# Row lists, gates and row stores of an attention, expert and dense chain rewritten; a third of a weight conversion moved to the expert stage

## The chip, the cores and the metric

The kernel runs on one core of one Trainium2 chip. The metric is the time of one execution on the device in microseconds (us); the median of three runs is 1482.52 us (1481.54 to 1482.77).

## The reference, cut to what matters

Three layers follow one another on 4 x 448 = 1792 tokens of 768 values (12 heads of 64): an attention whose heads are mixed before and after the softmax, a layer in which each token goes through one of eight experts, and a dense layer.

```python
scores = scale * q @ k.T                      # per batch and head
scores = einsum('bhij,hg->bgij', scores, w_pre)
attn = softmax(scores)                        # over j
attn = einsum('bhij,hg->bgij', attn, w_post)
x = (attn @ v) as rows of 768                 # 1792 rows
...
logits = xn @ en.T / tau                      # 8 experts, xn and en normalized
expert_idx = argmax(logits, axis=1)
gate_w = softmax(logits)[chosen]              # one number above 0 per token
for e in range(E):
    mask = expert_idx == e
    h = np.maximum(x[mask] @ w1[e], 0.0)
    out[mask] = gate_w[mask, None] * (h @ w2[e])
...
h = x @ w_in
g = h - np.tanh(h)
return g @ w_out
```

`w_in` and `w_out` come in 64-bit floats, so the kernel first makes 32-bit floats of them ("the conversion"). Nothing between gate and output of an expert depends on the gate but by a factor above 0, so a gate may also multiply x ahead of the two products.

## The kernel before, in words

All matrix products of the second and third layer run as three passes over a high and a low part ("h" and "l" tiles, split by an ACT copy and a subtraction), so each split costs one ACT and one DVE (or POOL) instruction. The order on every engine is the order of the program: the schedule is written out by hand, and each engine and each DMA queue (SP's, ACT's, POOL's) works through its list in order.

**Attention stage** (up to about 560 us). 180 blocks of ten rows by twelve heads are run through a loop of steps (L1122); a table of side work by step holds the loads, the transposes, the scores and the conversion. The conversion is cut into 96 pieces of 128 x 256 values (L106 to L134): one load by SP, three DVE instructions on the bits (L128 to L130), three POOL instructions (L131 to L133) and one store by SP. All 96 are in this stage (CONV_A = NCV, L113). x is stored to `x_d` in DRAM in the order in which the attention holds its rows (`emit_X`, L473); that order differs from the tokens', so the kernel keeps two numberings: `tokf` for gathering from `x_d`, `rowg` for the row of the output.

**Expert stage** (about 560 to 934 us). Nine items: experts 0 to 6, one overflow block of 128 tokens ("o"), expert 7 (L909). An expert takes up to 256 tokens. Each item n has a first half, eight chunks f of w1 (`h_chunk`, L787: 18 matmuls, then ACT's relu L796 and DVE's subtraction L797, in two PSUM banks by turns), and a second half, eight chunks of w2 (`y_turned`, L741: 18 matmuls each). After each chunk of the second half come pieces of a to-do list for item n+1 (L1214 to L1224): six splits of w1 (`do1`, L949, then L715 on ACT and L717 on DVE), then four transposes of gathered rows with their split (`xsplit`, L728: three PE transposes L732, ACT L735, DVE L736). The list is dealt out evenly over the chunks that are left. Chunk f also splits w2 chunk f+4 (`do2`, L954) ahead of the list. Four raw buffers of each weight are loaded ahead by SP.

Beside this, the generator `tables` (L915) is pumped a few steps per chunk (L1207 to L1210): first `emit_G` (L571, the gates), then `emit_ov` (L591), which computes each token's place in the list of tokens sorted by expert, sends row number and gate there by sixteen indirect DMAs of POOL into `sid_d` (L674 to L677), reads the list back by a DMA on ACT's queue (L680), makes `sid` and writes the gates in list order to `gat_d` (L687, ACT's queue too).

An item's result is copied by ACT into `yT` at a column that a register holds (`y_out_turned`, L770); the overflow block's goes through `y_out_tokens` (L774). Experts are written in ascending order, 256 columns each, so that what one writes too far the next overwrites.

**Dense stage** (about 934 us to the end). Two halves of 896 columns, each with eight groups of w_in and w_out. Ahead of a half, its columns are multiplied by their gates and split (`y_start`, `y_piece`, L1246 to L1258): a broadcast load of the gates from `gat_d`, and per piece of 128 x 448 the multiplication by POOL (or DVE, L1256), ACT's copy (L1257) and the subtraction (L1258). Twelve pieces run at the start of the stage, twelve spread over the last two groups of the first half. `stageA` (L1297) makes h and its function g with six ACT and DVE steps per tile (L1315 to L1329, POOL's L1295), `stageB` (L1335) the product with w_out, summed up by DVE in `acc` (L1352). The finished rows, 128 at a time, go to `out` by an indirect DMA of POOL (L1355), seven per half; each of them waits until the one before has landed, since any could write any row.

```python
            todo = []
            if not last:
                nw1, nx = [], xtile(f"i{n + 1}")
                todo = [lambda c=c: do1(n + 1, c, nw1) for c in range(KD)]
                todo += [lambda j=j, t=t, hf=hf: xsplit(nx, t, j, hf, f"i{n + 1}") for j, t in enumerate(nxg) for hf in range(2)]
            pts = y_banks(nm, 2 if e == OV else 3)
            for f in range(KF):
                (y_tokens if e == OV else y_turned)(pts, hhl, w2c[f], f)
                if f + W2B < KF:
                    do2(n, f + W2B, w2c)
                k_ = -(-len(todo) // max(1, KF - 1 - f))
                for fn in todo[:k_]:
                    fn()
                todo = todo[k_:]
```

Of the kernel before, what the change touches and what calls it, by code (L numbers as in the profile page):

```python
# [30 lines left out]
def body(ctx: ExitStack, tc, q, k, v, w_pre, w_post, emb, tau, w1, w2, win, wout, out):  # L31
# [42 lines left out]
    sid_d = dram.tile([NT, 2], F32, name="sid_d")  # L74
    gat_d = dram.tile([1, NT], F32, name="gat_d")
# [4 lines left out]
    rowg = persist.tile([128, 4 * B, 2], F32, name="rowg")  # L80
# [32 lines left out]
    CONV_A = NCV  # L113
# [24 lines left out]
    if True:  # L138
# [67 lines left out]
        for b in range(B):  # L206
            pool.iota(tokf[:, 4 * b:4 * b + 4], pattern=[[120, 4]], base=b * S, channel_multiplier=1,
                      allow_small_or_imprecise_dtypes=True)
        dve.tensor_copy(tokh, tokf)
# [17 lines left out]
        rg4 = rowg.rearrange("p (b t) o -> p b t o", b=B)  # L227
        dve.tensor_scalar(rg4[:, :, 0:3, 0], rowf[:, :, 0:3], rq[:, 1:2], None, ALU.add)
        dve.tensor_scalar(rg4[:, :, 3, 0], rowf[:, :, 3], rq[:, 3:4], None, ALU.add)
# [242 lines left out]

        def emit_X(T, hf, cpy=act.copy):  # L473
# [11 lines left out]
            def evac():  # L485
                cpy(xm[:n, hf * 384:(hf + 1) * 384].rearrange("p (c m) -> p c m", c=3), pv[:, :, 0:128])
                dve.reduce_sum(lg[:n, hf, T, :], pv[:, :, 128:136].rearrange("p c e -> p e c"), axis=AX.X)
                r0 = b * S + i0
                if T == 4 * B - 1:
                    act.dma_start(x_d[r0:r0 + n, hf * 384:(hf + 1) * 384], xm[:n, hf * 384:(hf + 1) * 384])  # L490
                elif hf:
                    sp.dma_start(x_d[r0:r0 + n, :], xm[:n])
# [78 lines left out]
        def emit_G():  # L571
# [16 lines left out]
            dve.tensor_copy(rowg[:, :, 1], gate)  # L588
            yield

        def emit_ov():  # L591
# [39 lines left out]
            dve.tensor_copy(z[:, 0:1], bs[:, 0, E - 1:E])  # L631
# [6 lines left out]
            bt = small([128, 4 * B, E], F32, "bt")  # L638
            bz = small([128, 2, 4 * B], F32, "bz")
            for x in range(2):  # L640
                dve.tensor_tensor(bt, ohk, bs[:, x:x + 1, 0:E].to_broadcast([128, 4 * B, E]), op=ALU.mult)
                yield
                dve.reduce_sum(bz[:, x, :], bt, axis=AX.X)
                yield
# [4 lines left out]
            yield  # L649

            dve.tensor_add(bz[:, 0, :], bz[:, 0, :], posk)
            yield

            lo = bz[:, 1, :]
            dve.scalar_tensor_tensor(lo, posk, -float(CAP), lo, ALU.add, ALU.add)
            yield
            ge = small([128, 4 * B], F32, "ge")
            dve.tensor_scalar(ge, lo, c0, mainc[:, E - 1:E], ALU.is_ge, ALU.mult)
            yield
            dve.tensor_add(lo, lo, ge)  # L660
            yield
            dve.tensor_scalar(lo, lo, z[:, 0:1], None, ALU.add)
            yield
            dve.tensor_sub(lo, lo, bz[:, 0, :])
            yield
            dve.tensor_scalar(ge, posk, float(CAP), None, ALU.is_ge)
            yield
            dve.tensor_mul(lo, lo, ge)
            yield
            spos = small([128, 4 * B], I32, "spos")  # L670
            dve.tensor_tensor(spos, bz[:, 0, :], lo, op=ALU.add)
            yield

            for t in range(4 * B):  # L674
                n = IT[t % 4][1]
                pool.indirect_dma_start(out=sid_d, out_offset=bass.IndirectOffsetOnAxis(ap=spos[:n, t:t + 1], axis=0),
                                        in_=rowg[:n, t, :], in_offset=None)  # L677
                yield
            sg = small([128, NT // 128, 2], F32, "sg")
            act.dma_start(sg, sid_d.rearrange("(t p) o -> p t o", p=128))  # L680
            yield
            dve.tensor_copy(sid, sg[:, :, 0])
# [9 lines left out]
    with mctx:  # L692
# [492 lines left out]
        for c in range(4, KD):  # L1185
            feed1(act)
# [265 lines left out]
```

## Time and profile before

| what | value |
|---|---|
| median of three runs | 1482.52 us |
| the profiled execution, its own time | 1482.83 us |
| its span in the profile | 1481.1 us |
| PE busy | 1326.2 us (90%) |
| DVE busy | 1004.2 us (68%) |
| ACT busy | 753.4 us (51%) |
| POOL busy | 514.8 us (35%) |
| mean granted clock of TensorE | 0.954 of full speed |

The span is what the profile covers; the execution's own time is 1.73 us longer. Busy shares are means over three stages with different limits. Clocks are shares of TensorE's full 2.4 GHz. Matmul records overlap, since the engine is pipelined: the distance of two starts is the time that one takes from the engine.

### The profile page before, as it was taken

Reading aid. Unit: us, or ns where it says so; the run is one execution under the profiler, and the core shown is the slowest. Engines: PE = TensorE matmul, PEld = TensorE weight load, DVE = VectorE, ACT = ScalarE, POOL = GpSimd, SP = SyncE. Lnnn points to the kernel's source line nnn. Section 1 sums busy time; section 2 is a strip of 40 time slices with the busy share of each in tenths; the row PEclk is TensorE's granted clock in tenths of the full one; section 3 lists DMA queues with packets and bytes.
Section 4 is the critical chain, followed back from the end, with each engine's and each line's share of the span. In section 5 each row is a group of like instructions: output and inputs, shape, how many; then the busy total and the mean of one; then the engine's idle time right before and its main releaser. Section 6 shows DMA issues by size and latency. Waiting matters only on the chain. (4 is left out here: it accounts for less than half of the span.)

```text
span 1481.1 us, 25663 instructions
## 1 busy us (share of the span) xinstructions
PE 1326.2 (90%) x9422; PEld 1151.0 (78%) x9422; DVE 1004.2 (68%) x2194; ACT 753.4 (51%) x1518; POOL 514.8 (35%) x537
## 2 busy tenths in 40 slices
PE   8989998998999987719999998689999888999994
PEld 5767766776676766719999988569999777999994
DVE  5877886787678765406555564288886758788883
ACT  6666655665666643404454464355444435544440
POOL 0434443444444331120000010454345445444432
PEclk9999999999999998959999999779999999999997
DMA  6765775677566453605655562112212012221101
GB/s 163 209 189 172 217 206 144 189 228 206 159 199 208 151 190 118 192 1 193 214 192 193 193 213 84 56 43 64 65 43 68 31 54 107 65 65 43 44 21 75
DMA packets 145606, 194.98 MB, mean 132 GB/s; under 512 B 57126, under 2 KB 109270, under 8 KB 145478
## 3 DMA queue, kind: packets, MB, share of 16 engines
q1 hardware_dynamic: 137040, 177.73, 39.5%
q0 software_dynamic: 2992, 12.21, 2.2%
q10 hardware_dynamic: 5446, 3.37, 0.8%
q8 instruction: 76, 1.25, 0.3%
q14 instruction: 52, 0.43, 0.1%
HBM read 131.12 MB, written 23.61 MB: 104 GB/s over the span
## 5 line engine op out<-in xcount | busy, mean ns | idle before, releaser
L430 PEld LDWEIGHTS T<-w,p 120*112 120x112 f32 (+1 forms) x1440 | 166.4, 177 | 66.9 <-issue 47.6
L430 PE MATMUL T<-w,p 120*112 120x120 f32 (+1 forms) x1440 | 185.9, 272 | 6.3 <-DVE w L408 3.0
L398 ACT ACTIVATE p<-P,mx 120x448 f32<-120x448 f32 x180 | 113.8, 632 | 110.7 <-DVE mx L405 99.9
L393 PE MATMUL P<-sr,wpre 120*120 120x448 f32 x360 | 167.2, 546 | 1.1 <-DMA sr<-ssb 0.8
L1346 PE MATMUL o<-woh,gh 128*128 128x384 f32 x448 | 151.6, 338 | 12.6 <-DVE acc L1352 12.6
L1309 PE MATMUL h<-yh,wih 128*128 128x448 f32 x384 | 147.7, 385 | 14.6 <-ACT yh L1257 12.8
L395 DVE TENSOR_REDUCE mx<-P 120x1 f32<-120x448 f32 x180 | 111.7, 621 | 68.5 <-PE P L393 67.1
L1295 POOL TENSOR_TENSOR gl<-th,gh 128x448 fp32r<-128x448 f32 x64 | 74.7, 1167 | 234.2 <-ACT gh L1294 196.3
L133 POOL TENSOR_TENSOR cm<-cm,ct 128x256 f32<-128x256 f32 x96 | 69.8, 728 | 246.3 <-DVE ct L130 212.6
L1348 PE MATMUL o<-woh,gl 128*128 128x384 f32 x448 | 151.1, 337 | 4.8 <-POOL gl L1295 4.8
L1347 PE MATMUL o<-wol,gh 128*128 128x384 f32 x448 | 150.5, 336 | 0.0
L1310 PE MATMUL h<-yT,wih 128*128 128x448 f32 x384 | 147.9, 385 | 1.0 <-POOL yT L1258 1.0
L793 PE MATMUL hi<-xhi,w1hi 128*128 128x256 f32 x384 | 110.1, 287 | 42.8 <-DVE hli L797 42.5
L1311 PE MATMUL h<-yh,wil 128*128 128x448 f32 x384 | 146.3, 381 | 2.2 <-POOL wil L1284 1.8
L1352 DVE TENSOR_TENSOR acc<-acc,o 128x384 f32<-128x384 f32 x196 | 106.7, 548 | 43.5 <-PE o L1348 43.5
L1315 ACT ACTIVATE u<-h 128x448 f32<-128x448 f32 x64 | 34.7, 543 | 175.6 <-PE h L1311 175.6
L750 PE MATMUL ypi<-hhi,w2hi 128*128 128x256 f32 x384 | 110.6, 288 | 0.0
L435 ACT COPY A<-T 112x480 f32<-112x480 f32 x180 | 101.4, 563 | 17.3 <-PE T L430 16.8
L794 PE MATMUL hi<-xli,w1hi 128*128 128x256 f32 x384 | 109.1, 284 | 0.0
L795 PE MATMUL hi<-xhi,w1li 128*128 128x256 f32 x384 | 108.8, 283 | 0.0
L752 PE MATMUL ypi<-hhi,w2li 128*128 128x256 f32 x384 | 108.7, 283 | 0.0
L751 PE MATMUL ypi<-hli,w2hi 128*128 128x256 f32 x384 | 108.5, 283 | 0.0
(272 smaller groups left out, 3358.8 us busy)
## 6 DMA issues: line engine op xcount, KB each, us to landing
sr<-ssb SPq DMA_DIRECT2D x176, 210.0 KB
r<-in_moe_w SPq DMA_DIRECT2D x72, 384.0 KB
r<-in_moe_w SPq DMA_DIRECT2D x52, 512.0 KB
craw<-in_moe_w_in SPq DMA_DIRECT2D x48, 256.0 KB
craw<-in_moe_w_out SPq DMA_DIRECT2D x48, 256.0 KB
raw<-wi_d SPq DMA_DIRECT2D x15, 768.0 KB
wor<-wo_d SPq DMA_DIRECT2D x15, 768.0 KB
wi_d<-cm SPq DMA_DIRECT2D x48, 128.0 KB
```

The lines of the kernel that those rows point to most:

```text
L393: pe.matmul(pt[:n, :S], wpre[:n, :n], t[:n, :], start=True, stop=True)
L395: dve.tensor_reduce(mx[:n, 0:1], pt[:n, :S], op=ALU.max, axis=AX.X, negate=True)
L398: return lambda: act.activation(p[:n, :], pt[:n, :S], AF.Exp, bias=mx[:n, 0:1], scale=1.0, accum_out=mx[:n, 1:2])
L430: pe.matmul(pt[:CP, c * n:(c + 1) * n] if m == 10 else pv[:, c], p[:n, c * CP:(c + 1) * CP], w[:n, :] if m == 10 else wv, start=True, stop ...
L750: pe.matmul(o, wh[:, sl], a, start=False, stop=False)
L793: pe.matmul(pt[:, :256], wh[:, sl], xh[:, c, :], start=c == 0, stop=False)
L1309: pe.matmul(pt[:, :S], wi[0][:, c, sl], yh[:, c, :], start=c == 0, stop=False)
L1310: pe.matmul(pt[:, :S], wi[0][:, c, sl], yl[:, c, :], start=False, stop=False)
L1311: pe.matmul(pt[:, :S], wi[1][:, c, sl], yh[:, c, :], start=False, stop=c == KD - 1)
L1346: pe.matmul(pt[:, :384], gh[:, sl], wo[0][:, f, n0:n0 + 384], start=f == 0, stop=False)
L1347: pe.matmul(pt[:, :384], gh[:, sl], wo[1][:, f, n0:n0 + 384], start=False, stop=False)
L1348: pe.matmul(pt[:, :384], gl[:, sl], wo[0][:, f, n0:n0 + 384], start=False, stop=f == GF - 1)
```

## The change

- **Row lists.** The sixteen indirect writes, the read back, `rowg`, `sid`'s conversion and the second numbering are gone. x is stored in the tokens' order (a store with a rearranged DRAM side, one more store for each fourth tile), so one list of indices serves gathers and outputs. Each item's list (256 or 128 row numbers, as integers) is written to `sid_d` by one DMA on ACT's queue at the item's column, after its result. `sid` is loaded from there by SP in the third group of the dense stage.
- **Gates.** They are stored in the tokens' order to `gate_d` by twenty DMAs on ACT's queue (elements of 4 bytes). For each item POOL gathers one gate per token (one or two indirect DMAs), and DVE multiplies the gathered x by it in place, ahead of the transposes: two instructions of 128 x 768 per expert, put in the to-do list between the six splits of w1 and the four `xsplit`. Expert 0 starts before the gates are there: its result waits in PSUM and is multiplied by a row of gates (turned by two matmuls) on the way to `yT`, by DVE, in the first half of item 1. The dense stage multiplies nothing.
- **Row stores.** The fourteen indirect stores go to views of `out` that are declared disjoint, so none waits for another.
- **Conversion.** 64 of the 96 pieces stay in the attention stage; 32 go to the first halves of the eight expert items, after chunks 1, 3, 5 and 7.
- The memory reserved for POOL's DMA descriptors is set to 8192 bytes a partition.

```diff
-    CONV_A = NCV
+    CONV_A = 64
...
+        def x_store(eng, T, xm, cs):
+            b, it = divmod(T, 4)
+            i0, n = IT[it]
+            r0, nb = b * S + i0, n // 10
+            eng.dma_start(x_d[r0:r0 + 10 * nb, cs].rearrange("(m r) d -> r m d", r=nb), xm[:10 * nb, cs])
+            if n % 10:
+                eng.dma_start(x_d[r0 + 10 * nb:r0 + n, cs], xm[10 * nb:n, cs])
...
             dve.reciprocal(gate, es)
             yield
-            dve.tensor_copy(rowg[:, :, 1], gate)
-            yield
+            yield
+            for T in range(4 * B):
+                bq, it = divmod(T, 4)
+                i0, n = IT[it]
+                r0, nb = bq * S + i0, n // 10
+                act.dma_start(gate_d[r0:r0 + 10 * nb].rearrange("(m r) o -> r (m o)", r=nb), gate[:10 * nb, T:T + 1])
+                if n % 10:
+                    act.dma_start(gate_d[r0 + 10 * nb:r0 + n], gate[10 * nb:n, T:T + 1])
+                if T % 4 == 3:
+                    yield
...
-            for t in range(4 * B):
-                n = IT[t % 4][1]
-                pool.indirect_dma_start(out=sid_d, out_offset=bass.IndirectOffsetOnAxis(ap=spos[:n, t:t + 1], axis=0),
-                                        in_=rowg[:n, t, :], in_offset=None)
-                yield
-            sg = small([128, NT // 128, 2], F32, "sg")
-            act.dma_start(sg, sid_d.rearrange("(t p) o -> p t o", p=128))
...
-            act.dma_start(gat_d.rearrange("o (t p) -> (o p) t", p=128), sg2)
...
+        def gates(idx, nm, xs):
+            g = mp[0].tile([128, 2], F32, tag="gx", name=f"gx{nm}", bufs=2)
+            for j, i in enumerate(idx):
+                pool.indirect_dma_start(out=g[:, j:j + 1], out_offset=None, in_=gate_d, in_offset=bass.IndirectOffsetOnAxis(ap=i, axis=0))
+            return g, [lambda j=j, t=t: dve.tensor_scalar(t, t, g[:, j:j + 1], None, ALU.mult) for j, t in enumerate(xs)]
...
+            act.dma_start(sid_d[bass.ds(col, 256)].rearrange("(j p) o -> p (j o)", p=128), ids[:, 2 * e:2 * e + 2])
...
+        def conv_step():
+            if ncv[0] < NCV:
+                conv_do(ncv[0], mq[0])
+                if ncv[0] + 3 < NCV:
+                    conv_load(ncv[0] + 3, mq[0])
+                ncv[0] += 1
...
+                    if n == 1 and f == 5:
+                        y_out_turned(p0, 0)
+                    if f % 2:
+                        conv_step()
                     if n < 4:
                         pump(5 if n else 8)
...
                 todo = [lambda c=c: do1(n + 1, c, nw1) for c in range(KD)]
+                if n == 0:
+                    g0[0] = gates(idx(0), "i0", [])[0]
+                todo += gates(idx(n + 1), f"i{n + 1}", nxg)[1]
                 todo += [lambda j=j, t=t, hf=hf: xsplit(nx, t, j, hf, f"i{n + 1}") for j, t in enumerate(nxg) for hf in range(2)]
...
-        def y_piece(bk, c, g, e0=pool, e1=dve):
+        def y_piece(bk, c, e1=dve):
             yh, yl = yTb[bk]
             y = yS[:, c, bk * S:(bk + 1) * S]
-            t = tmp("s2")
-            e0.tensor_tensor(t, y, g, op=ALU.mult)
-            act.copy(yh[:, c, :], t)
-            e1.tensor_sub(yl[:, c, :], t, yh[:, c, :].bitcast(F32))
+            act.copy(yh[:, c, :], y)
+            e1.tensor_sub(yl[:, c, :], y, yh[:, c, :].bitcast(F32))
...
-                    pool.indirect_dma_start(out=out, out_offset=bass.IndirectOffsetOnAxis(ap=sid[:, k:k + 1], axis=0),
+                    pool.indirect_dma_start(out=outv[k], out_offset=bass.IndirectOffsetOnAxis(ap=sid[:, k:k + 1], axis=0),
                                             in_=ac, in_offset=None)
...
+            if j == 2:
+                sp.dma_start(sid, sid_d[0:NT].rearrange("(t p) o -> p (t o)", p=128))
```

## Rows read from the trace of the kernel before

**Rows 1.** Stages: stretch, its length, busy us (instructions) per engine, clock, DMA share, GB/s.
```profile
core 0: us, PE busy (x) PEld busy (x) DVE busy (x) ACT busy (x) POOL busy (x), PEclk, DMA share, GB/s
300.00:450.00 150.00, 140.41 (x1227) 102.90 (x1226) 116.55 (x350) 94.37 (x224) 66.22 (x93) 1.00 0.67 198
...
760.00:840.00 80.00, 80.00 (x675) 79.84 (x673) 42.00 (x56) 41.03 (x66) 5.93 (x5) 1.00 0.57 201
...
619.99:661.42 41.43, 0.00 (x1) 0.00 (x1) 0.42 (x1) 0.38 (x1) 13.74 (x14) 0.56 0.05 10
661.42:670.00 8.58, 8.58 (x53) 8.40 (x54) 3.75 (x22) 1.15 (x3) 0.00 (x0) 0.75 0.20 2
```

**Rows 2.** Waits: engine and line, what ended them, us in total, times, longest.
```profile
ACT hhi L796 <- DMA sid_d<-rowg,spos: 43.6, 1, 43.6
...
POOL sid_d L676 <- DMA sid_d<-rowg,spos: 30.7, 15, 5.1
```

**Rows 3.** ACT's DMA queue in order of time: start us, us, what, how many.
```profile
664.11 0.38 ACTq L687 DMA_DIRECT2D gat_d<-sg  x1
...
935.62 0.83 ACTq L1249 DMA_DIRECT2D grow<-gat_d  x2
```

**Rows 4.** Second halves of items 2 and 5, in order of time, and one DVE group.
```profile
718.78 0.49 PE L732 MATMUL xti<-ident,xgi 128*128 128x128 f32 x3
...
720.90 0.95 DVE L717 TENSOR_TENSOR w2li<-r,w2hi 128x768 fp32r<-128x768 f32 x1
...
827.08 0.49 PE L732 MATMUL xti<-ident,xgi 128*128 128x128 f32 x3
...
829.50 0.95 DVE L717 TENSOR_TENSOR w2li<-r,w2hi 128x768 fp32r<-128x768 f32 x1
...
L715 DVE CAST w1hi<-r 128x1024 fp32r<-128x1024 f32 x4 | 2.7, 684 | 0.0
```

**Rows 5.** PE in order of time after a wait in the dense stage (the wait in brackets).
```profile
1255.43 0.69 PE L1348 MATMUL o<-woh,gl 128*128 128x384 f32 x1 [4.81 <-POOL gl L1295]
...
1259.83 0.36 PE L1311 MATMUL h<-yh,wil 128*128 128x448 f32 x1
```

**Rows 6.** The conversion's instructions: count, ns min/median/max, first and last start us.
```profile
L131 POOL TENSOR_TENSOR cm<-craw x96: 607/612/618, 46.0 to 504.8; 128x256 f32<-128x256 f32 x96
L132 POOL TENSOR_SCALAR cm<-cm x96: 846/847/977, 46.7 to 505.5; 128x256 f32<-128x256 f32 x96
L133 POOL TENSOR_TENSOR cm<-cm,ct x96: 722/727/737, 50.3 to 507.8; 128x256 f32<-128x256 f32 x96
...
L128 DVE TENSOR_SCALAR ct<-craw x96: 276/285/355, 48.9 to 506.5; 128x256 int32<-128x256 int32 x96
L129 DVE SCALAR_TENSOR_TENSOR ct<-craw,ct x96: 424/426/502, 49.3 to 506.8; 128x256 int32<-128x256 int32 x96
```

**Rows 7.** Groups by line, DVE in the dense stage: busy us, mean ns of one.
```profile
L1326 DVE SCALAR_TENSOR_TENSOR s<-s,u 128x448 f32<-128x448 f32 x64 | 72.9, 1139 | 0.4
...
L1327 DVE SCALAR_TENSOR_TENSOR s<-s,h 128x448 f32<-128x448 f32 x64 | 39.8, 621 | 2.2
```

**Rows 8.** Start of the dense stage, in order of time, and the gates' group.
```profile
936.49 0.40 ACT L1363 CAST wih<-raw 128x256 fp32r<-128x256 f32 x1 [2.30 <-issue]
...
940.81 0.74 PE L1309 MATMUL h<-yh,wih 128*128 128x448 f32 x1 [7.24 <-ACT yh L1257]
...
968.82 0.62 DVE L1324 TENSOR_TENSOR th<-h,th 128x448 f32<-128x448 f32 x1
...
L1256 POOL TENSOR_TENSOR s<-yT,grow 128x448 f32<-128x448 f32 x20 | 23.1, 1159 | 72.3 <-DMA grow<-gat_d 62.3 <-DVE yT L1258 9.9
```

**Rows 9.** Two stretches of the dense stage, columns as in the first group.
```profile
1146.00:1262.00 116.00, 98.61 (x476) 91.45 (x476) 79.48 (x128) 52.07 (x96) 57.94 (x46) 0.91 0.20 68
1300.00:1400.00 100.00, 100.00 (x536) 96.15 (x535) 85.56 (x131) 44.97 (x83) 44.77 (x30) 1.00 0.17 54
```

**Rows 10.** The end: DVE's last sum and POOL's last row store.
```profile
1462.18 0.56 DVE L1352 TENSOR_TENSOR acc<-acc,o 128x384 f32<-128x384 f32 x1 [0.49 <-PE o L1348]
...
1475.30 0.97 POOL L1355 DMA_INDIRECT out<-acc,sid  x1 [2.82 <-DMA out<-acc,sid]
```

More of the change, by code (lines that the diff above doesn't have):

```diff
@@ L6 @@
 from concourse._compat import with_exitstack
+from concourse.bass_types import dram_disjoint_views
 from concourse.masks import make_identity
@@ L893, in over_alone @@
             xgt = gather(oi, nm)
+            for fn in gates([oi], nm, [xgt])[1]:
+                fn()
             w1c = [split1(t, "w1", f"{nm}_{c}", KD) for c, t in enumerate(r1)]
@@ L956, in do2, with idx @@
             feed2()
+        def idx(n):
+            e = items[n]
+            return [osrc[2]] if e == OV else [ids[:, 2 * e + j:2 * e + j + 1] for j in range(2)]
         def gathers(n):
-            e = items[n]
-            ix = [osrc[2]] if e == OV else [ids[:, 2 * e + j:2 * e + j + 1] for j in range(2)]
-            return [gather(i, f"i{n}_{j}") for j, i in enumerate(ix)]
+            return [gather(i, f"i{n}_{j}") for j, i in enumerate(idx(n))]
+        ncv = [CONV_A]
+        def conv_step():
[4 more added lines that the diff above has]
+                ncv[0] += 1
         side = {}
@@ L1186, in body @@
             feed1(act)
+        for j in range(CONV_A, min(NCV, CONV_A + 3)):
+            conv_load(j, mq[0])
         for n, e in enumerate(items):
@@ L1225, in body @@
             if e == OV:
-                y_out_tokens(pts, col_reg(E), nm)
+                y_out_tokens(pts, col_reg(E), nm, osrc[2])
+            elif n == 0:
+                p0 = pts
             else:
-                y_out_turned(pts, col_reg(e))
+                y_out_turned(pts, e)
             if not last:
                 w1c, xhl = nw1, nx
+        while ncv[0] < NCV:
+            conv_step()
         nov = nc.values_load(ovi[0:1, 0:1], min_val=0, max_val=NOV)
@@ L1247, in y_start @@
             yTb[bk] = dp.tile([128, KD, S], F32R, tag="yh", name=f"yh{bk}", bufs=3), yS[:, :, bk * S:(bk + 1) * S].bitcast(F32R)
[L1248 to L1252 removed]
+            return [(bk, c) for c in range(KD)]
+        def y_piece(bk, c, e1=dve):
             yh, yl = yTb[bk]
             y = yS[:, c, bk * S:(bk + 1) * S]
[L1255 to L1258 removed]
+            act.copy(yh[:, c, :], y)
+            e1.tensor_sub(yl[:, c, :], y, yh[:, c, :].bitcast(F32))
         nb_ = [0]
@@ L1363, in body @@
             act.copy(wi[0][:, c], raw6[:, c])
-            y_piece(*y0[c], *((dve, pool) if c % 2 else (pool, dve)) if c < 4 else (dve, dve))
+            y_piece(*y0[c])
             pool.tensor_sub(wi[1][:, c], raw6[:, c], wi[0][:, c].bitcast(F32))
```

90 lines of the change are left out of this document (31 added, 59 removed).

## The prediction

> **What bounds the kernel now.** I read the stretches first. In the attention stage and in the middle of the expert stage PE is busy for 140.4 of 150 us and 80 of 80 us at full clock, while DVE has 42.0 of 80 us there [rows 1]: PE is the bound, and only what makes it wait, or adds to its work, counts. So the next view is PE in order of time, where it stands still. There are four places, all touched by the change.
>
> First, PE does nothing for 41.43 us from 619.99 [rows 1]. The view of waits says why: ACT sits 43.6 us until the last indirect write of the row list has landed [rows 2]. ACT's queue holds the read back of that list, the relus queue behind it, both PSUM banks fill, PE stops. The list takes so long because each of the sixteen writes waits for the one before: 30.7 us of waits at POOL [rows 2], and 13.74 us of issuing in that stretch [rows 1].
>
> Second, the dense stage starts slowly: PE's first matmul is at 940.81 after a wait of 7.24 us, and DVE comes to the first step of the function only at 968.82 [rows 8], since twelve pieces pass through gate, copy and subtraction one after another.
>
> Third, around the change of halves the clock is 0.91 and 476 matmuls take 116 us; later 536 take 100 us [rows 9]. 476 x 100 / 536 = 88.8, so 27 us are lost.
>
> Fourth, DVE's last sum is over at 1462.74, and POOL issues the last row store at 1475.30 [rows 10].
>
> **The change part by part**, against the profiled execution's own 1482.83 us.
>
> *The list at register offsets.* The 41.43 us go. With them goes the half clock behind: 8.58 us at 0.75 [rows 1], 2.1 us. Together **-43.5**. The new list is one DMA of ACT's per item, 0.38 us [rows 3], behind the copies to `yT`, where ACT has nothing due: 0; without that cover 9 x 0.38 = 3.4 us. The DVE steps that go are beside PE. What is late next in that place is the gates.
>
> *Storing the gates.* Twenty DMAs on ACT's queue, in the first half of item 0: five after chunk 1, fifteen after chunk 2. Two issues in a row took 0.83 us, so 0.42 each [rows 3] and 8.4 us for twenty; relus are queued behind them, and PE behind the relus. A chunk is 18 matmuls of 80 / 675 = 0.1185 us [rows 1], 2.1 us, and the second bank lets PE run one chunk ahead: 6.3 us are left. They come as two waits of three to four us, and after a wait of 4.81 us the chip's records show 0.38 us from start to start instead of 0.2 until 1259.83, twelve matmuls in 4.4 us [rows 5], 2 us lost. I take **+10**; 4 if two chunks hide it and the clock holds, 13 if nothing does.
>
> *Gates on gathered x.* This is the part that I expect to cost most, and it is a matter of order. POOL's gathers are free (POOL is busy 5.93 of 80 us [rows 1]). But DVE's multiplications stand in the list behind the six splits of w1, ahead of the transposes, which now read their result. With twelve entries in place of ten the list gives two each to chunks 0 to 4: splits, splits, splits, multiplications, transposes. On DVE the multiplications follow the split of the last w2 chunk, which ends at 720.90 + 0.95 = 721.85 in item 2 [rows 4]. One multiplication of 128 x 768 I bound from a cast of 128 x 1024 in 684 ns [rows 4], 0.51 us, and the conversion's one-input step, 285 ns for 256 columns [rows 6], 0.86 us; I take 0.65, nearer to the cast, whose length it is nearer to. So x is ready at 722.5. PE would be at that place when chunk 4 is done: its second transposes start at 718.78 [rows 4], right behind chunk 4 and, with the moved entry, 0.3 us sooner. It waits 4.0 us. In item 5 the same sum is 829.50 + 0.95 + 0.65 - 826.78 = 4.3 us [rows 4]. Transposes stand in PE's own queue, so nothing else runs in that time. Six hand-overs (items 0 to 5) at 4.2 us, and 2 us of half clock after each [rows 5], make 37.2; the two hand-overs around the overflow block, with one and two multiplications in another order, I put at 4 together. **+41**; 22 if half of the wait is caught up in DVE's queue and the clock holds, 55 if weights come later too.
>
> *Expert 0 late.* DVE's three products of 128 x 512 and a copy fall into the first half of item 1, with banks to spare: **+1**, between 0 and 3.
>
> *The conversion.* A piece is 0.285 + 2 x 0.426 = 1.14 us of DVE and 0.61 + 0.85 + 0.73 = 2.19 us of POOL [rows 6]. In the expert stage it is four pieces in a first half, 4.6 us on a DVE half idle, two DMAs each on SP between weight loads that are due a half later. SP's store waits for POOL, and loads of w2 queue behind it for some 3 us, which four buffers cover. **+3**, from 0 to 12 (a third of a chunk's DVE time each). In the attention stage PE's idle time is 9.6 of 150 us [rows 1], mostly waits for splits of k and q that stay: **-2**, from 0 to -8. POOL's 2.19 us per piece are off the path in both.
>
> On ports: DVE's step with two inputs in SBUF takes 1139 ns, the same size with one input from PSUM 621 ns [rows 7]. The Trainium skill, page "SBUF — State Buffer", section "Who interferes with whom", says that a DVE instruction with two SBUF inputs and a GpSimd instruction that reads SBUF exclude each other for a whole instruction; that is the rule that speaks against moving POOL's work beside the splits, and this trace agrees with it by those two rows. By the rule alone the moved POOL time would be DVE waiting, which is the second rival below.
>
> *Dense stage without gates.* A piece at the start was POOL 1.16, ACT 0.57, DVE 0.63 in a chain, some 2.4 us, and twelve fill 936.49 to 968.82 [rows 8]. Without the first link ACT's copies do not wait for anything, and PE's three matmuls at half clock (1.1 us) set the pace: about 13 us, so DVE's chain starts at 950 in place of 969. **-19**; -12.6 if only twelve links of 1.05 go, -25 if the 7.24 us go whole as well. At the change of halves twelve POOL products go, and the row stores of the first half no longer hold POOL's queue, in which one wait cost PE 4.81 us [rows 5]. DVE's subtractions stay, so I take 16 of the 27 us: **-16**, from -8 to -25.
>
> *The end.* The last store is issued behind DVE's last sum: 1475.30 - 1462.74 = **-12.6** [rows 10]; a store's landing is the same.
>
> Sum: -43.5 + 10 + 41 + 1 + 3 - 2 - 19 - 16 - 12.6 = -38 us, 1444.7 against the execution's own time; the median of the runs is 0.3 below that execution, so **1444 us**.
>
> **The rivals.**
> - *The gates are early.* If DVE's queue is ahead of PE (w1 splits sooner, since PE now waits elsewhere), the 41 us are not lost: 1403 us. For it: none of the transposes waits today. Against it: the DVE times above are those of a queue that runs without a gap.
> - *POOL locks DVE out (slower).* The place is the first half of each expert item, the price 32 x 2.19 = 70 us of POOL [rows 6], during which DVE's splits stand, as 1139 against 621 ns shows [rows 7]. If all of it reached PE: 1444 - 3 + 70 = 1511 us. It decides for slower once 41 of the 70 us reach PE. Against it: DVE has 38 of 80 us free [rows 1].
> - *The gate stores wait for one another (slower).* If each of the twenty waits for the landing of the one before, as the sixteen writes did, at 43.6 / 16 = 2.7 us [rows 2], they take 54 us on ACT's queue: 1444 - 10 + 54 = 1488 us. It takes over from 2.5 us each. Against it: their ranges are known when the program is built and do not overlap.
> - *The change does not do what it says:* stores to the views still wait. Then the 12.6 us stay, 1457 us.
>
> **How the numbers follow.** The forecast has 0.77, early gates 0.10, waiting views 0.06, POOL 0.04, serial gate stores 0.03. The terms' bounds around 1444, most of them independent, give 1420 to 1466, which takes in the waiting views; early gates (below) and the two slow cases (above) are left out. A measurement of this kernel tells 0.2%, about 3 us, from no change. Faster: the first three with a little off, 0.92; within 0.2%: 0.02; slower: 0.06.
>
> **What would show it.** No wait of 40 us on ACT or PE near 620; twenty short DMAs on ACT's queue near 580 and relus behind them; PE's transposes in each second half waiting some 4 us for DVE's multiplication, with a clock below 1 behind; DVE's first function step near 15 us after the first dense matmul; row stores at the end 1 to 2 us apart. I am wrong if the transposes do not wait, or if PE waits for subtractions in the first halves.

## The result, and the profile after

The changed kernel takes 1465.49 us (median of four runs, 1462.93 to 1469.09) beside 1482.6 us for the kernel before on the same chip: ratio 0.9888, 95% interval 0.9862 to 0.9914, 17 us faster. The forecast was 1444 us, 38 us faster. It lies within the range given, but more than half of the forecast gain is missing.

The profiled execution took 1462.93 us (span 1461.2 us, mean granted clock 0.96 of full speed), so the two traces differ by 19.9 us of span. The table splits them. A "first half" runs from an item's first matmul of the hidden layer to its first matmul of y, a "second half" from there to the next item's first matmul; all marks are starts of PE's matmuls. In the dense stage the marks compare the same matmul of the line that opens each group (L1309 before, L1321 after).

| stretch | before, us | after, us | difference | forecast |
|---|---|---|---|---|
| start to the first expert matmul | 566.76 | 560.00 | -6.8 | -2 |
| item 0, first half (gate stores) | 21.21 | 48.75 | +27.5 | +10 |
| item 1, first half (list stall before) | 60.60 | 22.72 | -37.9 | -42.5 (stall -43.5, expert 0 late +1) |
| the other six first halves | 102.2 | 102.3 | +0.1 | +3 (conversion) |
| seven second halves, overflow block in the last | 164.7 | 208.1 | +43.4 | +41 |
| last y matmul to the 161st dense one | | | -10.3 | -19 |
| around the change of halves, to the 257th | | | -24.4 | -16 |
| to PE's last matmul | | | +0.6 | 0 |
| PE's last matmul to the end | | | -12.2 | -12.6 |
| sum | | | -19.9 | -38.1 |

Three terms came out as forecast (the products, the end, and, but for 5 us, the stall that went). One row carries most of the miss: item 0's first half lost 27.5 us where 10 were forecast. Two more, the dense start and the change of halves, miss by about 8.5 us each in opposite directions.

Windows of the profile after, columns as in [rows 1]: two stretches in item 0's first half and one around the change of halves.

```profile
core 0: us, PE busy (x) PEld busy (x) DVE busy (x) ACT busy (x) POOL busy (x), PEclk, DMA share, GB/s
572.00:581.00 9.00, 4.21 (x18) 3.91 (x18) 2.27 (x8) 1.10 (x2) 0.57 (x1) 0.53 0.19 34
581.00:597.50 16.50, 0.00 (x0) 0.00 (x0) 0.42 (x1) 0.87 (x2) 0.00 (x0) 0.50 0.34 24
...
1162.00:1278.00 116.00, 114.25 (x607) 109.24 (x606) 104.79 (x152) 65.55 (x124) 56.34 (x42) 1.00 0.24 78
```

For 16.5 us no computing engine does anything to speak of, and the granted clock is at its lower level. The last row answers to [rows 9]: PE is busy 114 of 116 us at full clock, where it was 98.6 at 0.91.

The waits of the profile after (what waited, for what, us in total, times, longest); the first line is from the window of item 0's first half, the second from the whole expert stage:

```profile
ACT hhi L786 <- DMA gate_d<-gate: 24.2, 2, 19.7
...
PE xti L707 <- DVE xgi L698: 37.3, 8, 8.5
```

The 43.6 us of [rows 2] are gone, and in their place stand two waits that the change itself brought. In order of time, the profile after shows both, and then the dense start and the end (start, duration, what, how many, idle time before in brackets):

```profile
572.18 3.05 ACTq L598 DMA_DIRECT2D gate_d<-gate  x4
...
576.65 6.04 ACTq L598 DMA_DIRECT2D gate_d<-gate  x3
582.74 0.48 ACTq L600 DMA_DIRECT2D gate_d<-gate  x1
584.96 3.49 ACTq L598 DMA_DIRECT2D gate_d<-gate  x4
...
589.14 6.92 ACTq L598 DMA_DIRECT2D gate_d<-gate  x4
...
597.52 0.58 PE L783 MATMUL hi<-xhi,w1hi 128*128 128x256 f32 x1 [16.62 <-DVE hli L787]
...
715.85 0.95 DVE L683 TENSOR_TENSOR w2li<-r,w2hi 128x768 fp32r<-128x768 f32 x1
716.72 1.14 DVE L698 TENSOR_SCALAR xgi<-xgi,gxi 128x768 f32<-128x768 f32 x2
...
717.38 1.54 PE L707 MATMUL xti<-ident,xgi 128*128 128x128 f32 x6 [4.76 <-DVE xgi L698]
...
960.11 0.38 ACTq L761 DMA_DIRECT2D sid_d<-ids  x1
...
968.33 0.40 ACT L1377 CAST wih<-raw 128x256 fp32r<-128x256 f32 x1 [7.77 <-SPq L1248]
...
968.81 6.09 POOL L1379 TENSOR_TENSOR wil<-raw,wih 128x256 fp32r<-128x256 f32 x6 [23.88 <-ACT wih L1377]
969.23 6.15 DVE L1270 TENSOR_TENSOR yT<-yT,yh 128x448 fp32r<-128x448 f32 x6 [16.19 <-ACT yh L1269]
...
975.95 1.70 DVE L1270 TENSOR_TENSOR yT<-yT,yh 128x448 fp32r<-128x448 f32 x3 [0.56 <-ACT yh L1269]
...
983.11 0.61 DVE L1336 TENSOR_TENSOR th<-h,th 128x448 f32<-128x448 f32 x1
...
1453.24 0.96 POOL L1367 DMA_INDIRECT out<-acc,sid  x1 [1.12 <-DVE acc L1364]
...
1454.49 0.55 DVE L1364 TENSOR_TENSOR acc<-acc,o 128x384 f32<-128x384 f32 x1 [0.49 <-PE o L1360]
...
1455.32 0.96 POOL L1367 DMA_INDIRECT out<-acc,sid  x1 [1.12 <-DVE acc L1364]
```

The twenty gate stores occupy ACT's queue from 572.18 to 596.58, 24.4 us. Their issuing alone is 16 x 0.756 (median of L598) + 4 x 0.482 (L600) = 14.0 us, so 10 us are pauses between stores. At 716.72 the products stand right behind the split of w2, and PE's transposes behind them: the hand-over as forecast, with a wait of 4.76 us here. At the end the last store is 0.8 us behind the start of the last sum, where [rows 10] had 13.1.

What the pauses are is read from the built program. The DMAs that SP and ACT issue signal eight counters in turn, SP's and ACT's the same eight, and each of these stores but the first waits until the last DMA on its counter has landed. ACT's stores in the order of the program (number, line, what, what each waits for; rows left out in between):

```
633 L598 DMA gate_d<-gate 12x10x1 [waits DMAHW5_49]
...
641 L598 DMA gate_d<-gate 12x10x1 [waits DMAHW3_49]
642 L598 DMA gate_d<-gate 8x10x1 [waits DMAHW5_49]
```

Number 633 is the second store, issued at 572.99; 642 is the ninth, on the same counter. The trace shows the eighth issued at 577.45 and the ninth at 582.04, 9.05 us after the second; in the trace the last signal of the second's landing is at 582.02. So with eight stores in flight a store of 120 single values of 4 bytes takes about 9 us to land, and every later store waits for one of those eight. The store of 8 values issued at 575.27, in the midst of them, landed at 585.11, 9.84 us later, so a store's own number of values does not set its landing alone; what is on its way ahead of it is the likely rest.

### The profile page after: what moved, and what is told of

Same layout as the page of the kernel before. It is cut to its first block, busy times and chain, and to the rows that moved or that the text cites. A ratio compares the mean times of both kernels' runs of the same rounds, so it can differ in the third digit from the quotient of the medians.

```text
span 1461.2 us, 25689 instructions
## 1 busy us (share of the span) xinstructions
PE 1325.1 (91%) x9426; PEld 1160.8 (79%) x9426; DVE 1019.7 (70%) x2194; ACT 752.2 (51%) x1515; POOL 503.5 (34%) x512
## 5 line engine op out<-in xcount | busy, mean ns | idle before, releaser
L1321 PE MATMUL h<-yh,wih 128*128 128x448 f32 x384 | 142.7, 372 | 11.2 <-ACT yh L1269 9.3
L1323 PE MATMUL h<-yh,wil 128*128 128x448 f32 x384 | 143.2, 373 | 3.1 <-POOL wil L1296 3.1
L1322 PE MATMUL h<-yT,wih 128*128 128x448 f32 x384 | 142.8, 372 | 0.4 <-DVE yT L1270 0.3
L783 PE MATMUL hi<-xhi,w1hi 128*128 128x256 f32 x384 | 112.0, 292 | 25.6 <-DVE hli L787 24.7
L725 PE MATMUL ypi<-hhi,w2hi 128*128 128x256 f32 x384 | 114.6, 298 | 0.0
L726 PE MATMUL ypi<-hli,w2hi 128*128 128x256 f32 x384 | 112.4, 293 | 0.0
L727 PE MATMUL ypi<-hhi,w2li 128*128 128x256 f32 x384 | 112.3, 293 | 0.0
```

What stands on the lines that cost most here:

```text
L725: pe.matmul(o, wh[:, sl], a, start=False, stop=False)
L726: pe.matmul(o, wh[:, sl], l, start=False, stop=False)
L1321: pe.matmul(pt[:, :S], wi[0][:, c, sl], yh[:, c, :], start=c == 0, stop=False)
L1322: pe.matmul(pt[:, :S], wi[0][:, c, sl], yl[:, c, :], start=False, stop=False)
L1323: pe.matmul(pt[:, :S], wi[1][:, c, sl], yh[:, c, :], start=False, stop=c == KD - 1)
```

## The experiments

The kernel before, run beside each group, had medians of 1478.89 to 1481.48 us, so results are compared by their ratio to it; the changed kernel's is 0.9888.

**Gate stores on another queue.** Edit:

```
-                act.dma_start(gate_d[r0:r0 + 10 * nb]...
+                sp.dma_start(gate_d[r0:r0 + 10 * nb]...
```

> The twenty gate stores are issued by SP in place of ACT, nothing else differs from the changed kernel. Theory A (the relus of item 0 stand on ACT's queue behind the stores, and the stores wait for one another's landing): the first half of item 0 falls from 48.75 us to 22 to 25 us, ACT has no wait for a gate store, the time falls by some 24 us, to about 1441 us; SP's weight loads behind the stores may give up to 6 of it back. Rival B (that half is held by something else, such as DVE's steps between its chunks, and the stores only run beside it): the first half stays above 40 us and the time within 5 us of 1465.

Measured: 1459.58 us, ratio 0.9856 (0.9827 to 0.9884), and neither theory as it stood. Item 0's first half fell from 48.75 to 24.48 us, as A says, but its second half grew from 26.55 to 44.98. The waits of this run's item 0, SP's queue in the last line, the others all engines:

```profile
PE xti L707 <- DVE xgi L698: 24.3, 1, 24.3
ACT w1hi L681 <- DMA r<-in_moe_w: 22.0, 2, 21.1
...
SPq L598 <- DMA gate_d<-gate: 5.1, 4, 2.5
```

The relus did wait for ACT's queue. But SP needs nearly as long for the twenty stores, 20.7 us from 572.66 to 593.40, the later ones again waiting for earlier ones, and the weight loads queue behind them there: splits of w1 come 21 us late, the products behind them too. The Trainium skill, page "DMA: Bandwidth & Descriptors", section "Issuing engines are not separate DMA queues", says that starting DMAs from several engines saves only the time that a sequencer takes to start them. This run agrees: the stores take 20.7 us on SP for 24.4 on ACT. By the ratios some 5 us of the 27.5 are won (0.9856 for 0.9888), and the two intervals overlap.

**Fewer values per store.**

```
-  ... .rearrange("(m r) o -> r (m o)", r=nb), gate[:10 * nb, T:T + 1])
+  ... .rearrange("(m r) o -> r (m o)", r=nb)[0:1], gate[:10, T:T + 1])
...
+        sp.dma_start(gate_d.rearrange("(p t) o -> p (t o)", p=128), iota_s[:, :14])
```

> The twenty gate stores stay on ACT's queue, but the sixteen larger ones write ten gates each in place of 80 or 120; one early store fills the array with constants. Most gates are left out. Theory A (with at most eight stores in flight, the later ones wait for the landing of single values, which takes long by their number): the waits between the stores go, twenty issues of some 0.5 us stay, 10 us, and the first half of item 0 falls from 48.75 to 27 to 34 us. Rival B (a store lands after some 9 us whatever its size): stores from the ninth on still wait, and the first half stays above 40 us.

Measured: 1449.3 us, ratio 0.9806 (0.9778 to 0.9835). This kernel leaves most gates out, so only its times are of use. The first half is 31.7 us, as A says. ACT's queue of this run in order of time:

```profile
572.21 1.46 ACTq L598 DMA_DIRECT2D gate_d<-gate  x4
...
574.43 1.10 ACTq L598 DMA_DIRECT2D gate_d<-gate  x3
575.57 0.31 ACTq L600 DMA_DIRECT2D gate_d<-gate  x1
575.92 1.44 ACTq L598 DMA_DIRECT2D gate_d<-gate  x4
577.40 0.31 ACTq L600 DMA_DIRECT2D gate_d<-gate  x1
579.63 1.42 ACTq L598 DMA_DIRECT2D gate_d<-gate  x4
```

Twenty stores are out by 581.40, 9.2 us in place of 24.4, with one pause of 1.9 us. That pause is no store's doing: the store issued at 579.63 has the counter of a weight load that SP issued at 576.18 and that landed at 579.61. Issuing one of ten values takes 0.34 us (median) in place of 0.76. The second store, issued at 572.56, landed at 574.23, after 1.67 us in place of 9.0. So both the issue and the landing grow with the number of single values: of the 15.2 us saved, about 7 are issue and 8 are pauses. The Trainium skill, the same page, section "Latency and other measured facts", gives some 2 us as a DMA's fixed cost, most of it the round trip to the memory. The stores of ten values agree with it; with 120 values and eight in flight the landing took about 9 us, and the measurement decides.

**Gates stored as rows.** PE turns the 128 x 16 gates, DVE copies them into the order of tokens, and ACT stores rows of 120 or 88 adjacent gates:

```
+            pe.transpose(pg[:4 * B, :128], gate, ident)
...
+            for it in range(4):
...
+                act.dma_start(gate_d.rearrange("(b s) o -> b (s o)", b=B)[:, i0:i0 + n], (gA if it < 3 else gB)[it::4, :n])
```

> The gates are turned by one transpose of PE's and three copies of DVE's, and then stored by four DMAs of ACT's in place of twenty, as rows of 88 or 120 adjacent gates in place of single values. Theory A (the twenty stores cost by waiting for one another's landing, which is long for single values): the first half of item 0 falls from 48.75 us to 21 to 25, nothing waits for a gate store, item 0's second half stays at some 26 us, and the time falls by 23 to 28 us, to about 1440. Rival B (the cost is in any store of the gates at that place, by its bytes or by the transposition of their order): the first half stays above 30 us and the time above 1448.

Measured: 1447.82 us, ratio 0.9776 (0.9744 to 0.9808). The four stores take 2.5 us on ACT's queue, and none of them waits for another. But the first half is 29.95 us, between the theories: the transpose stood too early, and PE waited 4.44 us for DVE's gates. So the same with the transpose two chunks later (24 steps of the table in place of 8), nothing else:

> The changed kernel with the gates turned and stored by four DMAs, two chunks later than in the run with the turned gates; nothing else differs. Theory A (the gate stores are the 27.5 us but for some 3 us of the conversion's steps on DVE): item 0's first half falls from 48.75 to 21 to 24 us, and the time by 22 to 27 us, to about 1441. Rival B (what the stores delayed is late in any case, and comes back as a wait in item 0's second half and in item 1): the first half falls as much, the two after it grow by 5 us or more together, and the time stays at 1446 or above.

Measured: 1444.5 us, ratio 0.9757 (0.9729 to 0.9786). Item 0's first half is 22.3 us: the stores, issue and pauses together, were 26.5 of the 27.5 us. The four stores of rows landed 2.0 to 2.8 us after their issue. The time fell by 1.3% of 1480, about 19 us, less than A and more than B: item 1's first half is 4.1 us shorter too, but the second halves together are 11.6 us longer than in the changed kernel, 5 of them around the overflow block. The products there wait as before, for 47.9 us in place of 37.3: part of what PE wins is waited away at the next product.

**Products earlier in the list.**

```
-                todo += gates(idx(n + 1), f"i{n + 1}", nxg)[1]
+                todo[2:2] = gates(idx(n + 1), f"i{n + 1}", nxg)[1]
```

> The gate multiplications stand in the list of each second half behind the second split of w1 in place of the sixth; nothing else differs. Theory A (the transposes wait only because of the order in DVE's queue): PE's wait for DVE's product, 37.3 us in 8 waits, falls below 8 us, the second halves of items 0 to 5 go from 24.8 to 26.6 us back to 19 to 21, and the time falls by 30 to 40 us, to about 1430 us. Rival B (DVE is full in that half, and the 1.14 us of products delay whatever stands behind them): the wait moves to the w1 splits or the subtractions of x, and the time falls by 0 to 15 us, to 1450 or more.

Measured: 1427.34 us, ratio 0.9622 (0.9585 to 0.9659): theory A. The waits of PE in the expert stage of this run:

```profile
PE xti L707 <- DVE xli L711: 11.4, 3, 4.0
...
PE xti L707 <- DVE xgi L698: 2.9, 2, 1.5
```

The second halves of items 1, 2, 4 and 5 are 19.2 us. Those of items 0 and 3 keep 24.7 and 26.3: there the transposes wait for subtractions of x. One moved line gives 2.7% of the time, though DVE does the same work in both kernels.

**The last list write early.** In the last item the write of the list goes ahead of the second half:

```
-            act.dma_start(sid_d[bass.ds(col, 256)]..., ids[:, 2 * e:2 * e + 2])
+            if e < E - 1:
+                act.dma_start(sid_d[bass.ds(col, 256)]..., ids[:, 2 * e:2 * e + 2])
...
+            if last:
+                act.dma_start(sid_d[bass.ds(col_reg(e), 256)]..., ids[:, 2 * e:2 * e + 2])
             pts = y_banks(nm, 2 if e == OV else 3)
```

> The row list's last write is issued ahead of the second half of the last item in place of behind its copies to yT; nothing else differs. Theory A (the loop behind the last item lets ACT go on only when that write, issued at 960.11, has landed, at 968.33): PE's gap ahead of the dense stage falls from 9.31 to 3 to 4 us, and the time by 5 to 7 us, to about 1459. Rival B (the loop's entry itself costs it): the gap stays at 8 to 10 us and the time within 2 us of 1465.

Measured: 1458.26 us, ratio 0.9835 (0.9809 to 0.9861): theory A. From this run's trace, in order of time:

```profile
964.56 0.40 ACT L1380 CAST wih<-raw 128x256 fp32r<-128x256 f32 x1 [1.76 <-issue]
...
965.48 0.47 PE L1324 MATMUL h<-yh,wih 128*128 128x448 f32 x1 [3.31 <-ACT yh L1272]
```

The wait ahead of the dense stage is 3.31 us in place of 9.31. In the changed kernel the loop behind the last item let ACT go on only when the write of 256 single values, issued at 960.11, had landed: the last signal of its landing is at 967.57, and ACT's next work starts at 968.33.

**Row stores to the whole output again.** `out=outv[k]` becomes `out=out`.

> The row stores of the dense stage write the whole output again in place of its disjoint parts; nothing else differs. Theory A (each store waits for the one before, at the end 12.2 us, and at the change of halves one wait of 4 to 5 us, while most of the 24.4 us gained there came from POOL's twelve products): the time rises by 14 to 20 us, to about 1482. Rival B (the stores are the whole of the change of halves): the time rises by 30 us or more, to 1496 or above.

Measured: 1480.54 us, ratio 1.0007 (0.9988 to 1.0026): theory A. The last five stores of this run:

```profile
1460.36 0.96 POOL L1367 DMA_INDIRECT out<-acc,sid  x1 [2.82 <-DVE acc L1364]
1464.15 0.96 POOL L1367 DMA_INDIRECT out<-acc,sid  x1 [2.83 <-DMA out<-acc,sid]
1467.93 0.96 POOL L1367 DMA_INDIRECT out<-acc,sid  x1 [2.82 <-DMA out<-acc,sid]
1471.72 0.96 POOL L1367 DMA_INDIRECT out<-acc,sid  x1 [2.83 <-DMA out<-acc,sid]
1475.51 0.96 POOL L1367 DMA_INDIRECT out<-acc,sid  x1 [2.82 <-DMA out<-acc,sid]
```

Each waits for the landing of the one before, 3.79 us apart, where the views let them go 2.08 us apart. (Where the line names DVE's sum, that sum had long been done: the last of all is over at 1462.22.) The change of halves still gains 19.0 us in this run, so about 5.3 of the 24.4 us were the stores'. The rest, by elimination, belongs to the gate products that left the dense stage; no run puts these back.

**Conversion back in the attention stage.** `CONV_A = 64` becomes `CONV_A = NCV`.

> All 96 pieces of the conversion are in the attention stage again; nothing else differs. Theory A (the 32 pieces cost nothing in the expert stage and 6.8 us in the attention stage): the first expert matmul comes at 566 to 568 us in place of 560.0, the first halves of items 2 to 6 stay at 17.0 us, and the time rises by 6 to 8 us, to about 1472. Rival B (POOL's and DVE's steps of the conversion hold DVE up in the expert stage, so part of the lost time there is theirs): the first or second halves of items 0 to 5 get shorter by 1 us or more each, and the time stays or falls, to 1465 or below.

Measured: 1463.57 us, ratio 0.9874 (0.9851 to 0.9897), the same as the changed kernel within the noise: rival B, but only in items 0 and 1. The first expert matmul is back at 567.1, 7.1 us later; the first halves of items 0 and 1 are 4.5 and 3.5 us shorter, and those of items 2 to 6 stay at 17.03.

**Together.** Gates turned, products behind the second split, last list write early:

> Gates turned and stored by four DMAs, products behind the second split, last list write early: three edits together. Theory A (they are separate losses): the gains add, 26 + 38 + 7 us, to about 1394. Rival B (two of them hide behind one another, as the gates on SP moved the loss to the next half): above 1405.

Measured: 1405.22 us, ratio 0.9503 (0.9462 to 0.9544). This is the early transpose, whose 4.42 us of waiting is in it. The time stands at the bound of rival B, yet most adds up: by their ratios the three edits gained 17, 39 and 8 us alone, 64 in sum, and 57 together. Then the gates of items 1 and later gathered at the start of the item before, and the products behind the first split (`todo[1:1]`):

> As the three edits together, but the gates of item 1 and later are gathered at the start of the item before, and the products stand behind the first split. Theory A (the waits left in the run with the products behind the second split, in the second halves of items 0 and 3 and around the overflow block, come from the order of DVE's queue): item 3's second half falls from 26.3 to 19.2 us, and the time to 8 us under that of the three edits. Rival B (they come from weights that arrive late): the same within 3 us.

Measured: 1401.68 us, ratio 0.946 (0.9428 to 0.9492). Item 3's second half went from 24.25 to 21.13, not to 19.2, and item 0's grew by 1.3: in between. Then the transpose two chunks later:

> As the three edits with the early gather, but the transpose of the gates is issued two chunks later in item 0. Theory A (PE's wait of 4.57 us for the gates, and the half clock behind it, are all that is left of the gate stores): item 0's first half falls from 28.8 to 21 to 24 us, and the time by 4 to 7 us, to about 1396. Rival B (the gates then land too late for the products of item 0's second half, which is 25.8 us long there): that half grows by 4 us or more and the time stays within 2 us of 1402.

Measured: 1397.17 us, ratio 0.9438 (0.9412 to 0.9465): theory A, with 22.2 us for item 0's first half, though its second half grew by 2.0; item 1's first half is 4.3 us shorter and item 2's 4.5 longer, and the intervals of the two runs overlap. And the entries that turn x put between the splits of w1:

```
+                for i_, fn in enumerate(xs):
+                    todo.insert(3 + 2 * i_, fn)
```

> As the run before it, and the four entries that turn the next x stand between the splits of w1 in place of behind them. Theory A (PE's waits of 4.67, 1.72 and 5.29 us for the subtractions of x, and the half clock behind them, come from the place of these entries in DVE's queue): the waits go, and the time falls by 8 to 14 us, to about 1385. Rival B (the splits that now come later are the next bound): PE waits at the first matmuls of the next item, and the time stays within 4 us of the run before it, or rises.

Measured: 1391.72 us, ratio 0.9405 (0.9383 to 0.9428), 5 us, less than A. The waits for subtractions went, but in item 0 one of 5.99 us for the product took their place, and the overflow block kept 4.5 us in three waits.

**The conversion again, with the gates out of the way.** The run with the later transpose, and `CONV_A = NCV`:

> As the run with the later transpose, but all 96 pieces of the conversion in the attention stage. Theory A (the 32 pieces cost 8 us in items 0 and 1 only because the tables and the gate stores kept DVE and ACT full there): the attention stage is 7 us longer, the first halves are less than 3 us shorter, and the time rises by 4 to 7 us against the run with the later transpose. Rival B (they cost as much there as they save, whatever the gates do): the time stays within 2 us.

Measured: 1386.25 us, ratio 0.9367 (0.9344 to 0.9391): 11 us faster, which neither theory gave. The first halves are 6.5 us shorter together, the second halves 11.4 (8.2 of them in item 0), against 7.9 us at the start. In order of time, first the run with the pieces in the expert stage, then, in the last line, the run without them:

```profile
585.31 0.75 POOL L133 TENSOR_TENSOR cm<-cm,ct 128x256 f32<-128x256 f32 x1 [3.60 <-DVE bs L630]
586.20 1.06 POOL L701 DMA_INDIRECT gxi<-gate_d,ids  x1
...
593.38 0.62 DVE L702 TENSOR_SCALAR xgi<-xgi,gxi 128x768 f32<-128x768 f32 x1 [4.41 <-DMA gxi<-gate_d,ids]
...
587.38 0.97 POOL L701 DMA_INDIRECT gxi<-gate_d,ids  x1 [18.99 <-DMA gate_d<-gB]
```

POOL's step of the conversion waits for DVE, which is behind with the tables, and the gather of the gates stands behind it in POOL's queue. It comes 27.3 us after the item's first matmul (at 558.93), and DVE then waits 4.41 us for it with the splits of w1 behind. Without the pieces the gather comes 20.6 us after it, right behind the landing of the gate stores at 586.60. With the pieces these had landed by 581.35, 4.9 us ahead of the gather, so POOL's queue held it and not the stores. To split this further, x turned between and all pieces in the attention stage, and the same with 16 pieces in items 4 to 6 and the last:

```
-    CONV_A = 64
+    CONV_A = 80
...
-                    if f % 2:
+                    if f % 2 and n >= 4:
                         conv_step()
```

> Later transpose, early gather, x turned between the splits, and all 96 pieces of the conversion in the attention stage. Theory A (the two edits meet different waits): 4 us less than the run with the later transpose and the conversion back, about 1382. Rival B (with the conversion away no transposes wait any more, so their place is worth nothing): the same within 2 us, 1386.

> As the run with x turned between the splits, but 16 pieces of the conversion in the expert stage in place of 32, in items 4 to 6 and the last. Theory A (the pieces cost only where DVE also has the tables, in items 0 to 3): the halves of items 0 to 3 are as short as without any piece (20.2, 19.6, 17.5 and 19.3 us in items 0 and 1), those of items 4 to 6 stay at 16.9 and 19.2 us, half of the 7.9 us of the attention stage is kept, and the time is 3 to 4 us below the run with all pieces in the attention stage. Rival B (a piece costs wherever it stands): the same as that run or slower.

Measured: 1383.65 us, ratio 0.9355 (0.9327 to 0.9383), and 1382.87 us, ratio 0.9347 (0.932 to 0.9373). The first is 2.6 us below the run before it, between its theories, and the intervals overlap. The second is the same as the first within their intervals, yet not for rival B's reason: its halves are as short as without pieces (19.77 and 19.18 us in item 0, 16.89 in the first halves of items 4 to 6, 19.17 and 19.16 in the second halves of items 4 and 5), so sixteen pieces cost nothing there. The attention stage ends 3.1 us sooner, but PE then waits 7.46 us for the gathered x in place of 5.11. Why that gather lands later was not settled. These two are the fastest versions, 6.5% below the kernel before.

## Why the prediction was right or wrong

**The step that failed is "Storing the gates"**, put at +10 with bounds of 4 and 13; it measured 27.5 us, of which 26.5 went when the stores were replaced. Two figures in it were wrong. The issue of a store was taken from a DMA of another shape, 0.42 us [rows 3]; it is 0.76 for 120 single values and 0.34 for ten. And the stores were taken to be free of one another; the rival that made them wait had 0.03, argued down because their ranges do not overlap. They wait all the same, not for their ranges but for one of eight counters, from the ninth store on. The rival's price, 54 us, was too high for that reason: eight are in flight at a time. The truth lies between forecast and rival, and the upper bound, "13 if nothing does", was a bound of one figure, not of the mechanism. One of the prediction's own signs of being wrong came up here: in item 0's first half PE waited 6.26 and 16.62 us for DVE's subtractions, which waited for relus behind the stores.

**Gates on gathered x** was right, term and reason: +43.4 for +41, waits of 3.9 to 4.85 us at PE in items 0 to 5 for 4.2, and 6.2 us around the overflow block for 4. A product took 0.61 us, 0.65 was assumed. That the cause is the order of the list is shown by the moved line, which gave 33.8 of the 43.4 us back. One reading was wrong: the prediction says that none of the transposes waited before, but two did, 2.42 us at 687.02 and 3.70 at 894.56, for subtractions of x. The rival of early gates (0.10) describes the kernel with that line moved, not this one.

**The list.** The stall and the half clock went. Item 1 gained 37.9 us, since its first half is still 5.7 us over the 17.03 of later items; 3.5 us of that go when the conversion is taken out, and 4.1 when the gate stores are replaced, so the two overlap.

**The conversion.** +3 and -2 were forecast, and the net of about +1 agrees with what taking it out showed (2 us less, within the noise), but as a difference of larger parts: 7 us won in the attention stage, 8 lost in items 0 and 1. Something covered it: in the kernel with the gates turned, the products moved, the gates gathered early and the list written early, the 32 pieces cost 18 us in the expert stage. Which of these edits took the cover away is not shown. The rival of POOL locking DVE out did not decide: by the rows above, the loss runs through the order of DVE's and POOL's queues, and DVE's splits of w2 take 979 ns on average with the pieces beside them (28 splits up to 700 us in the run with the later transpose) and 954 with the pieces back in the attention stage. The Trainium skill, page "SBUF — State Buffer", section "Who interferes with whom", says that a DVE instruction with two SBUF inputs contends with a GpSimd (POOL) instruction that reads SBUF. This is visible at the dense start: DVE's six subtractions take 6.15 us, 1.03 each, while POOL's six run beside them, and 0.57 each (1.70 for three, at 975.95) without POOL. The rows [rows 7] bear it out too once they are split: of the 64 steps with two SBUF inputs, the nine that had no POOL instruction beside them took 0.62 us, and the 39 that had one for most of their time took 1.23 on average; with an input from PSUM all took 0.62.

**Dense start** (-19, measured -10.3). The chain was right: from the first dense matmul to DVE's first function step 13.9 us, 28.0 before, and 13 were assumed. The wait ahead of it was wrong: by the prediction's sum it was to shrink from 7.24 to about 3.5 us, and it grew to 9.3, since the new list write is the last thing before the loop and took 7.5 us to land. "ACT has nothing due: 0" overlooked the loop as one who waits. With the write issued early the wait was 3.3 us.

**Change of halves** (-16, measured -24.4, bound -25): the direction held, but the forecast kept 11 us for DVE's subtractions, and nearly all of it went: before, PE waited seven times there for over 0.3 us, 17.2 us in all (12.3 for DVE's sums, 4.81 for POOL), after it twice, 1.8 us. How much of that was the products' is not shown, as said at the run with the stores to the whole output. **The end** (-12.6, measured -12.2) was right to a row. **Attention stage** (-2, measured -6.8): PE's idle time there was partly the conversion's after all; putting the pieces back cost 7.1 us.

## What to carry to other kernels

Look at a small DMA's shape before pricing it: single 4-byte values from many partitions are slow to issue and slow to land, and the number of DMAs that may be in flight turns the landing into a queue; turn the data first and store rows. An operation added to a chain costs by its place in the other engine's queue, not by its duration: 1.14 us of products cost 6 us per item, and one moved line gave most of it back. Ask of work that seems free what covers it, and price it again when that cover is taken away: here the conversion went from nothing that could be measured to 11 us net.

## What the runs showed of the hardware that was not expected

A store of 120 single values was issued in 0.76 us, of 80 in 0.66, of ten in 0.34, and of 8 in 0.48 or 0.31. With eight in flight a store of 120 landed after about 9 us, one of ten after 1.7; a lone write of 256 values took 7.5 us to land and held a loop some 6 us longer than an early one. SP's and ACT's DMAs share eight counters here, so a store of one can wait for a weight load of the other, as it did for 1.9 us in the run with few values. Four stores of four rows, 88 or 120 gates a row, took 0.6 us each to issue, landed after 2.0 to 2.8 us and did not wait for one another.
